# Four column tiles of 128 and one store for the output of a gated attention and feed-forward decode kernel

## The chip, the cores and the metric

The kernel runs on one core of one Trainium2 chip. The metric is the device time of one execution in microseconds (us). Most executions of one kernel agree within 0.3%, so a change of 0.2 us in 197 can be told only from several rounds in which both kernels run on the same chip, and from the durations inside a trace. "Slow state" means an execution in which the records show a lower granted TensorE clock over the whole span and a longer time; here it happened once (217.08 us at a mean clock of 0.585). The granted clock is the share of full speed at which TensorE was allowed to run.

The engines are TensorE (PE; its weight loads are listed as PEld), VectorE (DVE), ScalarE (ACT), GpSimd (POOL) and SyncE (SP). SP and ACT also issue DMAs; their sequencers are listed as SPq and ACTq. Sixteen DMA engines move the data.

## The reference, cut to what matters

Four tokens (one per batch entry) go through two paths, which are mixed by a gate.

```python
def reference(A_x, A_k_cache, A_v_cache, A_wq, A_wo, B_x, B_W_gate, B_W_up, B_W_down, gate_w):
    x = A_x                                            # [4, 1, 512] bfloat16
    g = _sigmoid((x * gate_w).sum(-1, keepdims=True))
    a = _A_ref(x, A_k_cache, A_v_cache, A_wq, A_wo)    # 32 heads of 128 over the last 4096 keys; o @ wo, wo [4096, 512]
    b = _B_ref(x, B_W_gate, B_W_up, B_W_down)          # (relu(gate) * up) @ W_down, W_down [1792, 512]
    return g * a + (1 - g) * b                         # [4, 1, 512]
```

The kernel reads 81 MB (64 MB of it keys and values) to produce 4 KB of output. The parts that matter here are the last two products, `h @ W_down` and `o @ wo`. They are summed in the same PSUM accumulator, whose 4 x 512 results are cast to bfloat16 and stored.

## The kernel before: the parts that the change touches

The loads are issued by SP in one order: query weights, keys and values of eight sets, gate and up weights, the last values, down weights, and at the end the 4 MB of `wo` in six pieces. The 512 output columns are cut in two tiles of 256. Tile j is computed in TensorE's columns 64j and lands in partitions 64j to 64j+3. Both tiles run side by side.

```python
WO_PIECES = ((0, 8), (8, 16), (16, 24), (24, 28), (28, 30), (30, 32))   # 3 x 1 MB, 512 KB, 2 x 256 KB
OUTT = 2
OW = 512 // OUTT          # 256 columns of a tile
OR = 128 // OUTT          # tile j at partition 64*j

def store(E, e, t):       # tile t: 4 neighbouring partitions, 4 rows of 512 B
    E.op(lambda: e.dma_start(out.rearrange("b o d -> (b o) d")[:, OW * t:OW * t + OW], osum[OR * t:OR * t + 4, :]),
         ev=("OUT", t), waits=[("OSUM",)], ctr=f"d_out{t}")

# ... cut ...  TensorE: FFN (down projection) and WO (output projection) into bank ACC
def WO(p):
    lo, hi = WO_PIECES[p]
    w = [("WO", p)] + [("E", "OQ", g) for g in range(2)]
    for i in range(lo, hi):
        for j in range(OUTT):
            mm(banks[ACC][OR * j:OR * j + 4, 0:OW], oq[:, i, :], Wo[:, i, OW * j:OW * j + OW], False, i == 31,
               ev=..., waits=w if (i, j) == (lo, 0) else (), pos=(0, OR * j))

# ... cut ...  VectorE, last instruction
def FIN():
    E.op(lambda: v.tensor_copy(osum[:, :], banks[ACC][:, 0:OW]), ev=("OSUM",), waits=[("WOP", len(WO_PIECES) - 1)])

# ... cut ...  SP stores tile 0, ACT stores tile 1
```

## Time and profile before

| before | us |
|---|---|
| time, median of 3 runs | 197.54 |
| last `wo` load lands | 192.84 |
| last four matmuls | 192.89 to 193.27 |
| cast to `osum` | 193.31 to 193.74 |
| stores land (trace's increments): SP's, ACT's | 194.95, 195.13 |
| span ends | 195.59 |

The page of the kernel before shows what bounds it. Its third part lists the DMA queues with packets, MB and their share of the time of sixteen engines; its fourth part is the chain of work that ended last.

```profile
## 3 DMA queue, kind: packets, MB, share of 16 engines
q1 hardware_dynamic: 3904, 81.01, 97.1%
...
DMA 54%; DVE 30%; PE 9%; issue 5%; SPq 1%; ACT 0%
```

The load queue fills 97.1% of sixteen DMA engines' span. There is hardly any room in front of the last load, so what a change of the output path can win lies behind it. The end of the chain of waits in the same run, in order of time (start, duration, what), shows that part:

```profile
173.35 19.49 DMA slots<-in_A_wo_dram
192.84 0.04 issue
192.89 0.40 PE bank L320 x4
193.29 0.02 issue
193.31 0.42 DVE osum L576
```

The chain stops at the cast. The stores follow in the timeline of the same run (start, duration, engine, line, instruction). For a DMA the duration is the time the sequencer needs to issue it:

```profile
193.77 0.29 SPq L249 DMA_DIRECT2D out_dram<-osum  x1
193.77 0.62 ACTq L249 DMA_DIRECT2D out_dram<-osum  x1
```

Both stores are alike, and ACT takes twice as long to issue its one. So after the last load there are 2.75 us: 0.47 to the cast, 0.43 of cast, 1.39 to the last store's landing, 0.46 to close the program.

One more thing is read from the trace's packet records. Each DMA increments its semaphore once for each engine that takes part. For the last piece of `wo` these increments come in two groups:

```text
increments of the last piece, us after the first (190.98):
0.00 0.05 0.10 0.17 0.26 0.28 0.29 0.47 0.48 0.57 | 1.44 1.62 1.70 1.74 1.76 1.87
```

Six engines are late. Five 16 KB instruction fetches before the end (at 39, 72, 111, 146 and 183 us) each hold one engine for 0.92 to 1.06 us, and after each fetch one more engine is late in every later load. The sixth late engine appears after a single 8 KB fetch at 64 us. The loads are cut evenly, so nothing gives that time back. A load is complete when its slowest engine is.

### The profile page before, as it was taken

To read this page: it belongs to the slowest core of one execution; us is meant where nothing else is said; L and a number is where in the kernel's file an instruction comes from. 1 tells how busy PE (TensorE), PEld (TensorE's weight loads), DVE (VectorE), ACT (ScalarE), POOL (GpSimd) and SP (SyncE) were. 2 spreads that over 40 slices of the span, in tenths; PEclk is the share of its full clock that TensorE was granted. 3 is DMA by queue.
4 is the path that set the end of the run, shared out by engine and by line. 5 is a ranking of instruction groups with operands and counts; after the bars stand their busy time and mean duration, and the time that the engine had idled before them with its cause. 6 is when DMAs were issued, how large, how long until landed. Compare 5 with 4: busy or idle time off the path is not lost.

```text
span 195.6 us, 1780 instructions
## 1 busy us (share of the span) xinstructions
PE 121.2 (62%) x741; PEld 50.9 (26%) x741; DVE 124.0 (63%) x153; ACT 27.3 (14%) x33; POOL 9.5 (5%) x25
## 2 busy tenths in 40 slices
PE   0418279465933894595468953893395557734954
PEld 0213123122411331142113521241141112412631
DVE  6104769999299819971998199819972997460000
ACT  2213000040130013001300131014001400420100
POOL 7830000000000000000000000000000000000000
PEclk9999957999999697999886999699999789997999
DMA  6999999999999999999999999999999999999991
GB/s 221 442 423 436 429 442 436 419 436 429 436 456 429 437 426 436 429 429 429 436 429 436 426 429 429 429 429 429 429 426 429 429 405 434 448 429 403 417 402 53
DMA packets 3919, 81.12 MB, mean 415 GB/s; under 512 B 572, under 2 KB 584, under 8 KB 968
## 3 DMA queue, kind: packets, MB, share of 16 engines
q1 hardware_dynamic: 3904, 81.01, 97.1%
q8 instruction: 6, 0.10, 0.2%
q14 instruction: 1, 0.01, 0.0%
q10 hardware_dynamic: 8, 0.00, 0.0%
HBM read 81.01 MB, written 0.00 MB: 414 GB/s over the span
## 4 chain that ended last, share of the span: by engine, by line
DMA 54%; DVE 30%; PE 9%; issue 5%; SPq 1%; ACT 0%
DMA slots<-in_A_k_cache_dram 38%; DVE kt L492 21%; DMA slots<-in_A_wo_dram 10%; PE bank L320 7%; DMA gwT<-in_gate_w_dram 6%; DVE sc L528 5%; DVE qblk L518 1%; SPq L256 1%; DVE pT L543 1%; PE bank L324 1%; DVE rd L532 1%; ACT gwB L598 0%; DVE negmax L538 0%; DVE oq L555 0%; DVE osum L576 0%
## 5 line engine op out<-in xcount | busy, mean ns | idle before, releaser
L492 DVE STREAM_TRANSPOSE kt<-slots 128x2048 f32<-128x2048 f32 x32 | 73.7, 2304 | 27.5 <-DMA slots<-in_A_k_cache_dram 27.5
L320 PE MATMUL bank<-kt,qblk 128*128 128x512 bf16 x256 | 71.4, 430 | 29.2 <-DVE kt L492 29.1
L320 PEld LDWEIGHTS bank<-kt,qblk 128*128 128x128 bf16 x256 | 24.9, 106 | 70.7 <-DVE kt L492 37.6
L320 PE MATMUL bank<-slots,pT 128*64 128x512 bf16 x256 | 32.0, 407 | 5.7 <-DMA slots<-in_A_v_cache_dram 5.7
L617 ACT ACTIVATE pe<-sc,negmax 128x2048 bf16<-128x2048 bf16 x8 | 16.0, 2002 | 60.3 <-DVE negmax L538 60.3
L528 DVE CUSTOM_DVE_ANT_0 sc<-bank,maskf 128x512 bf16<-128x512 f32 x32 | 21.1, 658 | 4.1 <-PE bank L320 4.1
L320 PEld LDWEIGHTS bank<-slots,pT 128*64 128x64 bf16 x256 | 15.0, 117 | 23.1 <-issue 13.1
L543 DVE STREAM_TRANSPOSE pT<-pe 128x2048 bf16<-128x2048 bf16 x8 | 18.5, 2312 | 2.2 <-ACT pe L617 2.2
L602 ACT ACTIVATE osb<-bank 128x512 bf16<-128x512 f32 x8 | 4.8, 597 | 81.5 <-PE bank L320 81.5
L320 PE MATMUL bank<-rd,grpb 128*128 128x32 bf16 x8 | 1.5, 192 | 21.0 <-DVE rd L532 19.3
L555 DVE TENSOR_TENSOR oq<-bank,recip 64x128 bf16<-64x128 f32 x2 | 0.9, 442 | 11.5 <-PE bank L320 11.4
L320 PEld LDWEIGHTS bank<-rd,grpb 128*128 128x128 bf16 x8 | 0.8, 97 | 24.7 <-DVE rd L532 22.7
L320 PE MATMUL bank<-slots,oq 128*4 128x256 bf16 x64 | 4.3, 272 | 2.6 <-DMA slots<-in_A_wo_dram 1.9
L496 DVE COPY xT<-bank 128x16 bf16<-128x16 bf16 x1 | 0.2, 167 | 8.2 <-PE bank L324 8.2
L320 PE MATMUL bank<-slots,xT 128*4 128x512 bf16 (+1 forms) x64 | 5.2, 483 | 0.0
L576 DVE CAST osum<-bank 128x256 bf16<-128x256 f32 x1 | 0.4, 425 | 6.5 <-PE bank L320 6.5
L518 DVE TENSOR_SCALAR qblk<-bank 32x64 uint32<-32x64 uint32 x16 | 2.9, 215 | 2.3 <-PE bank L324 2.2
L320 PE MATMUL bank<-maskr,maskl 128*128 128x512 bf16 x1 | 0.6, 609 | 5.9 <-POOL maskr L296 5.9
L324 PE MATMUL bank<-identb,xsb 4*128 4x4 bf16 x4 | 0.3, 166 | 5.4 <-DMA xsb<-in_A_x_dram 5.4
L320 PEld LDWEIGHTS bank<-slots,oq 128*4 128x4 bf16 x64 | 2.3, 83 | 4.4 <-DMA slots<-in_A_wo_dram 3.1
L296 POOL TENSOR_SCALAR_AFFINE_SELECT fold<-fold 128x256 bf16<-128x256 bf16 x8 | 3.3, 417 | 1.1
L487 DVE MEMSET qblk<- 128x2304 uint32 x1 | 2.0, 1978 | 1.4 <-PEq L640 1.4
(58 smaller groups left out, 42.2 us busy)
## 6 DMA issues: line engine op xcount, KB each, us to landing
slots<-in_A_k_cache_dram SPq DMA_DIRECT2D x8, 4096.0 KB, 25.2
slots<-in_A_v_cache_dram SPq DMA_DIRECT2D x8, 4096.0 KB, 30.6
slots<-in_A_wq_dram SPq DMA_DIRECT2D x1, 4096.0 KB, 12.4
slots<-in_A_wo_dram SPq DMA_DIRECT2D x3, 1024.0 KB, 16.4
slots<-in_B_W_gate_dram SPq DMA_DIRECT2D x1, 1792.0 KB, 19.7
slots<-in_B_W_up_dram SPq DMA_DIRECT2D x1, 1792.0 KB, 23.6
slots<-in_B_W_down_dram SPq DMA_DIRECT2D x1, 1792.0 KB, 18.6
slots<-in_A_wo_dram SPq DMA_DIRECT2D x1, 512.0 KB, 19.2
```

The costliest lines, as they stand in the source:

```text
L256: E.op(lambda: e.dma_start(dst, src), ev=ev, waits=waits, ctr=ctr)
L296: op(lambda: e.affine_select(dst, src, pattern, cmp, fill, base=base, channel_multiplier=mult), ev)
L320: E.op(lambda: t.matmul(out_, lhsT, rhs, start=start, stop=stop, tile_position=pos, skip_group_check=True), ev=ev, waits=waits)
L324: E.op(lambda: t.transpose(out_, in_, idn), ev=ev, waits=waits)
L487: E.op(lambda: v.memset(qblk[:, :, :, :, :].rearrange("p s h c e -> p (s h c e)"), 0.0), ev=("QZ",))
L492: E.op(lambda: v.transpose(kt[:, f, :].bitcast(FP32), slot("k", s)[:, 4096 * f:4096 * f + 4096].bitcast(FP32)), ev=("E", "KT", s, f), waits=w)
L518: E.op(lambda dst=dst, r=r, g=g: v.tensor_scalar(dst, src[r, g, 0:B, :, :], 0, None, op0=ALU.bitwise_or), ev=("E",) + keys[1] if (q, g) == ...
L528: E.op(lambda: v.tensor_tensor_reduce(sc[:, 512 * f:512 * f + 512], banks[scb(key)], R["maskf"][:, :], 1.0, -3.0e38, ALU.add, ALU.max, mx4 ...
L532: E.op(lambda: v.tensor_tensor(rd32[:, :, :], bc(R["own8"][:, :].unsqueeze(2), 2, 4), bc(mx4[:, :].unsqueeze(1), 1, 8), ALU.mult), ev=("MA ...
L543: E.op(lambda: v.transpose(pT[:, s % 2, :], pe[:, :]), ev=("E", "PT", s), waits=[("EXP", s)] + ([("PV", s - 2)] if s >= 2 else []))
L602: E.op(lambda: a.activation(osb[:, s % 4, :], ob(s), ACTF.Copy), ev=("NORM", s), waits=[("PV", s)] + ([("OQ", 0)] if s >= 4 else []))
L617: E.op(lambda: a.activation(pe[:, :], sc[:, :], ACTF.Exp, bias=negmax[:, s % 2:s % 2 + 1], scale=SCALE, accum_out=rowsum[:, s:s + 1]), ev= ...
```

## The change

The intent: shorten everything behind the last load. Four column tiles of 128 columns make the last matmuls and the cast half as wide. The rows of a tile lie 8 partitions apart, so that all 16 rows have one step (`osum[0:128:8]`) and a single store takes them. The last 64 KB of `wo` are loaded in rows of 123, 3 and 2, numbers that three, three and two DMA engines can share, so that the late engines have nothing to do with them. The rest follows from it: one second-level head sum instead of two, memsets for the unused columns, bfloat16 constants.

```diff
-WO_PIECES = ((0, 8), (8, 16), (16, 24), (24, 28), (28, 30), (30, 32))
-OUTT = 2
+OUTT = 4
 OW = 512 // OUTT
 OR = 128 // OUTT
+ST = OR // B
+LW = 3 * ST + 2
+WO_PIECES = ((0, 32), (32, 64), (64, 96), (96, 112), (112, 120), (120, 126), (126, 128))
+LOW3 = (0, 123, 126, 128)
@@ loads
-                load(("WO", it[1]), f"d_wo{it[1]}", Wo[:, lo:hi, :], A_wo.rearrange("(p i) c -> p i c", i=32)[:, lo:hi, :],
-                     waits=w)
+                wo = A_wo.rearrange("(p i) c -> p (i c)", i=32)
+                for n, r in enumerate(wo_rows(it[1])):      # last piece: rows 0:123, 123:126, 126:128
+                    load(("WO", it[1], n), f"d_wo{it[1]}", Wo[r, OW * lo:OW * hi], wo[r, OW * lo:OW * hi], waits=w)
@@ stores
-        for t in range(0, OUTT, 2):
-            store(E, e, t)
-        E.wait([("OUT", t) for t in range(OUTT)])
+        load(("OUT",), "d_out", out.rearrange("b o (t c) -> t (b o) c", t=OUTT),
+             osum[0:128:ST, :], waits=[("OSUM",)])
+        E.wait([("OUT",)])
@@ TensorE
-                    mm(banks[ACC][OR * j:OR * j + 4, 0:OW], R["hg"][:, i, :], Wd[:, x:x + OW], i == 0, False,
+                    mm(banks[ACC][OR * j:OR * j + LW, 0:OW], R["hg"][:, i, :], Wd[:, x:x + OW], i == 0, False,
-            for i in range(lo, hi):
-                for j in range(OUTT):
-                    mm(banks[ACC][OR * j:OR * j + 4, 0:OW], oq[:, i, :], Wo[:, i, OW * j:OW * j + OW], False, i == 31,
+            for x in range(lo, hi):
+                i, j = x // OUTT, x % OUTT
+                mm(banks[ACC][OR * j:OR * j + LW, 0:OW], oq[:, i, :], Wo[:, OW * x:OW * x + OW], False, i == 31,
@@ cut: one OQ and EOQ pair instead of two, memsets of hg and oq, ee and e4 in BF16, ACT's store removed
```

More of the change, by code (lines that the diff above doesn't have):

```diff
@@ L116, in _alloc @@
     sb("gwT", [128, 4], BF16)
-    sb("osb", [128, 4, 512], BF16)
-    sb("oq", [128, 32, 4], BF16)
+    sb("osb", [128, NSET, 512], BF16)
+    sb("oq", [128, 32, LW], BF16)
     sb("identb", [128, 128], BF16)
@@ L121, in _alloc @@
     sb("ones", [128, 128], FP32)
-    sb("ee", [16, 128], FP32)
-    sb("e4", [16, 128], FP32)
+    sb("ee", [16, 128], BF16)
+    sb("e4", [16, 128], BF16)
     sb("rfold", [128, 128], FP32)
@@ L136, in _alloc @@
     sb("rowsum", [128, NSET], FP32)
-    sb("recip", [128, 2, 4], FP32)
+    sb("recip", [128, 4, 4], FP32)
     sb("ge", [128, 2, 4], FP32)
@@ L140, in _alloc @@
     sb("gg", [128, 2, 4], FP32)
-    sb("hg", [128, 14, 4], BF16)
+    sb("hg", [128, 14, LW], BF16)
     sb("osum", [128, OW], BF16)
@@ L150, in _order @@
     for s in range(1, NSET):
-        o += [("KT", s, 0), ("SC", s - 1, 3)] + [("RS", 0), ("OQ", 0)] * (s == 5) + [("SW", s - 1)]
+        o += [("KT", s, 0), ("SC", s - 1, 3)] + [("RS", 0)] * (s == 5) + [("SW", s - 1)]
         o += [("KT", s, 1), ("PT", s - 1), ("SC", s, 0), ("KT", s, 2), ("SC", s, 1), ("KT", s, 3)]
@@ L154, in _order @@
     s = NSET - 1
-    o += [("SC", s, 3), ("SW", s), ("PV", s - 1), ("PT", s), ("RS", 1), ("GU",), ("PV", s), ("FFN",), ("OQ", 1)]
+    o += [("SC", s, 3), ("SW", s), ("PV", s - 1), ("PT", s), ("RS", 1), ("GU",), ("PV", s), ("FFN",), ("OQ",)]
     return o + [("WO", p) for p in range(len(WO_PIECES))]
@@ L207, in _program @@
     Wd = slot("wd")[:, 0:14 * 512]
-    Wo = slot("wo", 0).rearrange("p (i c) -> p i c", i=32)
+    Wo = slot("wo", 0)
     grelu, hrow, hT = sc[:, 0:448], sc[:, 512:960], sc[:, 1024:1472]
@@ L240, in sc_free, with wo_rows @@
         return [("E",) + sck[n]] if n >= 0 else [("INIT",)]
+    def wo_rows(p):
+        return [slice(a, b) for a, b in zip(LOW3, LOW3[1:])] if p == len(WO_PIECES) - 1 else [slice(0, 128)]
     def set_of(s):
@@ L246, in ob @@
         return banks[OB[s % 2]]
-    def store(E, e, t):
-        E.op(lambda: e.dma_start(out.rearrange("b o d -> (b o) d")[:, OW * t:OW * t + OW], osum[OR * t:OR * t + 4, :]),
-             ev=("OUT", t), waits=[("OSUM",)], ctr=f"d_out{t}")
     def sync(e):
@@ L310, in gpsimd @@
         aff(R["own8"][:, :], R["own8"][:, :], [[16, 8]], 15, ge_, 0.0, ("OWN", 1), mult=-1)
+        op(lambda: e.memset(R["hg"][:, :, :], 0.0), ("HG0",))
+        op(lambda: e.memset(oq[:, :, :], 0.0), ("OQ0",))
         op(lambda: e.memset(R["fold"][:, :, :, :], 0.0), ("FOLD0",))
@@ L393, in PV, with OQ @@
                        (f, c) in ((3, 12), (3, 14)), ev=("PV", s) if (f, c) == (3, 14) else None, waits=w, pos=(0, r))
-        def OQ(g):
-            key = ("OQ", g)
-            r = 64 * g
+        def OQ():
+            key = ("OQ",)
             for t in range(2):
@@ L402, in OQ @@
                         first, lastmm = (t, cc, c) == (0, 0, 0), (t, cc, c) == (1, 1, 3)
-                        mm(banks[tr(key)][r:r + 64, 0:128], R["fold"][:, 2 * cc + t, c, :], osb[:, :, x:x + 32], first,
-                           lastmm, ev=key if lastmm else None, pos=(0, r),
-                           waits=tr_free(key) + [("NORM", 4 * g + 3), ("FOLD", 7)] if first else ())
+                        mm(banks[tr(key)][0:64, 0:256], R["fold"][:, 2 * cc + t, c, :], osb[:, :, x:x + 32], first, lastmm,
+                           ev=key if lastmm else None, pos=(0, 0),
+                           waits=tr_free(key) + [("NORM", NSET - 1), ("FOLD", 7)] if first else ())
         def GU():
@@ L426, in WO @@
             lo, hi = WO_PIECES[p]
-            w = [("WO", p)] + [("E", "OQ", g) for g in range(2)]
-            for i in range(lo, hi):
-                for j in range(OUTT):
-                    mm(banks[ACC][OR * j:OR * j + 4, 0:OW], oq[:, i, :], Wo[:, i, OW * j:OW * j + OW], False, i == 31,
-                       ev=("WOP", p) if (i, j) == (hi - 1, OUTT - 1) else None, waits=w if (i, j) == (lo, 0) else (),
-                       pos=(0, OR * j))
+            w = [("WO", p, n) for n in range(len(wo_rows(p)))] + [("E", "OQ")]
+            for x in range(lo, hi):
+                i, j = x // OUTT, x % OUTT
+                mm(banks[ACC][OR * j:OR * j + LW, 0:OW], oq[:, i, :], Wo[:, OW * x:OW * x + OW], False, i == 31,
+                   ev=("WOP", p) if x == hi - 1 else None, waits=w if x == lo else (), pos=(0, OR * j))
         fns = dict(CONST=CONST, XT=XT, Z=Z, Q=Q, QT=QT, SC=SC, PV=PV, SW=SW, RS=RS, OQ=OQ, WO=WO, GU=GU, FFN=FFN)
@@ L470, in _program @@
         elif k == "OQ":
-            dve.append(("EOQ", it[1]))
+            dve.append(("EOQ",))
     dve.append(("FIN",))
@@ L547, in ERS, with EOQ @@
             key = ("RS", g)
-            E.op(lambda: v.reciprocal(recip[:, 0, :], banks[tr(key)][:, 0:4]), ev=("E",) + key, waits=[key])
-            E.op(lambda: v.tensor_tensor(recip[:, 1, :], recip[:, 0, :], gg[:, 0, :], ALU.mult), ev=("RG", g),
+            E.op(lambda: v.reciprocal(recip[:, 2 * g, :], banks[tr(key)][:, 0:4]), ev=("E",) + key, waits=[key])
+            E.op(lambda: v.tensor_tensor(recip[:, 2 * g + 1, :], recip[:, 2 * g, :], gg[:, 0, :], ALU.mult), ev=("RG", g),
                  waits=[("E",) + key, ("G",)])
-        def EOQ(g):
-            key = ("OQ", g)
-            r = slice(64 * g, 64 * g + 64)
-            E.op(lambda: v.tensor_tensor(oq[r, :, :].rearrange("p i b -> p b i"),
-                                         banks[tr(key)][r, 0:128].rearrange("p (b i) -> p b i", b=4),
-                                         bc(recip[r, 1, :].unsqueeze(2), 2, 32), ALU.mult), ev=("E",) + key,
-                 waits=[key, ("RG", g)])
+        def EOQ():
+            key = ("OQ",)
+            for g in range(2):
+                r = slice(64 * g, 64 * g + 64)
+                E.op(lambda g=g, r=r: v.tensor_tensor(
+                    oq[r, :, 0:LW:ST].rearrange("p i b -> p b i"),
+                    banks[tr(key)][0:64, 128 * g:128 * g + 128].rearrange("p (b i) -> p b i", b=4),
+                    bc(recip[0:64, 2 * g + 1, :].unsqueeze(2), 2, 32), ALU.mult), ev=("E",) + key if g else None,
+                    waits=[key, ("RG", 1), ("OQ0",)])
         def H():
@@ L570, in EHT @@
             E.op(lambda: v.transpose(hT, hrow), ev=("HT",), waits=[("H",)])
-            E.op(lambda: v.tensor_tensor(R["hg"][:, :, :], hT.rearrange("p (i b) -> p i b", b=32)[:, :, 0:4],
+            E.op(lambda: v.tensor_tensor(R["hg"][:, :, 0:LW:ST], hT.rearrange("p (i b) -> p i b", b=32)[:, :, 0:4],
                                          bc(gg[:, 1, :].unsqueeze(1), 1, 14), ALU.mult), ev=("E", "HT"),
-                 waits=[("HT",), ("G",)])
+                 waits=[("HT",), ("G",), ("HG0",)])
         def FIN():
@@ L601, in NORM @@
         def NORM(s):
-            E.op(lambda: a.activation(osb[:, s % 4, :], ob(s), ACTF.Copy), ev=("NORM", s),
-                 waits=[("PV", s)] + ([("OQ", 0)] if s >= 4 else []))
+            E.op(lambda: a.activation(osb[:, s, :], ob(s), ACTF.Copy), ev=("NORM", s),
+                 waits=[("PV", s)])
         def GE():
@@ L622, in scalar @@
             fns[it[0]](*it[1:])
-        for t in range(1, OUTT, 2):
-            store(E, a, t)
     return [("tensor", tensor), ("vector", vector), ("scalar", scalar), ("gpsimd", gpsimd), ("sync", sync)]
```

## The prediction

> **What bounds the kernel.** The DMA stream: the page's queue section gives the load queue 97.1% of sixteen engines' span. The chain that ended last, from 165 us on, is 62.9% output-weight loads. Compute hides behind the loads, so only the tail can change:
> - The last output-weight piece lands at 192.84 (chain of waits).
> - Four matmuls of 256 columns: 192.89 to 193.27, 0.40 in the chain.
> - The output cast, 128x256: 193.31, 0.42.
> - Two stores from 193.77: issue 0.29 on SP, 0.62 on ACT. In the trace's DMA increments SP's lands at 194.95, ACT's at 195.13. The span ends at 195.59.
>
> **How the stream ends.** The last piece's increments come in two groups: ten engines at 190.98 to 191.55, six at 192.42 to 192.85. In the packet records each 16 KB instruction fetch (39, 72, 111, 146, 183 us) holds one engine 0.9 to 1.05 us; after it one more engine is late in every later load. So ten engines idle about 1.3 us at the end.
>
> **What the change does there.**
> 1. Rows of 123, 3, 2. The Trainium skill ("DMA: Bandwidth & Descriptors", why a DMA increments its semaphore by 16) says the engine count is the largest number up to 16 that divides the slowest dimension, lowest-numbered engines first. So 123 rows go to three engines, 41 rows of 512 B each, then three, then two. No run shows this yet. The other thirteen lose 4 KB each: eight packets shrink from 2048 B (80 ns apart) to 1536 B (about 61 ns), 0.15 us. The three get about 43 packets at an estimated 22 to 28 ns, about 1 us, into 1.3 us of slack, if they are early engines. My packet matching suggests so, not surely.
> 2. Last piece: two matmuls of 128 columns side by side instead of two pairs of 256. The second pair starts 105 ns after the first; a 128-column one lasts 219 ns in the trace: 0.16 less.
> 3. Cast of 128 columns instead of 256, at about 1 ns each: 0.13 less.
> 4. One store, not two: ACT's landed 0.19 after SP's. Against it: 16 rows of 256 B, and the skill's page (Specifications) warns of read-modify-write below 512 B. Net 0.07 less.
>
> **What is added off the critical path.** FFN and output matmuls double (28 to 56, 64 to 128). Gate and up projections ran four column tiles with starts 3 ns apart, 189 ns per group of 448 columns, so four at 128 columns should cost 56 to 90 ns against 108 for today's pair. The merged head fold costs 0.8 more, its second scaling 0.44; output matmuls still start near 188 and catch up before the third piece lands at 190.34. Three more load issues (0.43 each) hide behind 19 us of queueing; constants and memsets come early.
>
> **Sum.** 0.15 + 0.16 + 0.13 + 0.07 = 0.5 us less: 197.05 us (196.6 to 197.65). Faster over 2%: 1%; within 2%: 97%; slower: 2%.
>
> **What would show it.** Last landing near 192.7; last matmuls about 0.23; cast about 0.29; one store; increments of the last piece from three engines only, none later than the six late ones.
>
> **What would make it wrong.** The three being late ones, or 512-byte packets slower than 28 ns: the last landing moves up to 1 us. More TensorE instructions bring the next fetch forward (191.5 to about 189); on one of the three or on a late engine it costs up to 1 us. Slow 256-byte writes eat the store's gain.

## The result, and the profile after

The changed kernel took 197.64 us (median of 6 runs, 197.58 to 197.86), the kernel before 197.47 us in the same rounds (197.31 to 197.91). The ratio is 1.0006 with a 95% interval of 0.9993 to 1.0019. Ratios in this document are made from the fast runs of both kernels in the same rounds. They are not quite the ratio of the medians quoted; the plain means of the listed times give the same within 0.0005. In a second series of 5 rounds the ratio was 1.0015 (1.0002 to 1.0027). So there is no gain. If anything the change costs 0.1 to 0.3 us, and the time lies at the very upper end of the predicted range (197.64 of 197.65).

The page after shows the stream as it was:

```profile
## 3 DMA queue, kind: packets, MB, share of 16 engines
q1 hardware_dynamic: 4052, 81.01, 96.8%
```

The end of the chain of waits of the changed kernel:

```profile
172.57 19.33 DMA slots<-in_A_wo_dram
191.90 0.04 issue
191.95 0.61 PE bank L326 x16
192.56 0.01 issue
192.57 0.40 PE bank L326 x8
192.97 0.03 issue
193.00 0.45 PE bank L326 x8
193.45 0.02 issue
193.47 0.29 DVE osum L582
```

The cast fell from 0.42 to 0.29 as intended. But the matmuls before it take 0.45, not less than the 0.40 of before, and eight of them wait for the last landing, not two. Then the store, from the timeline:

```profile
193.79 0.67 SPq L259 DMA_DIRECT2D out_dram<-osum  x1
```

Its issue takes 0.67 where SP's plain store took 0.29. Laid out from the landing of the last down weights, which both kernels load alike, the tails are as follows (from the traces' increments and instruction times; the second run of the changed kernel is the control of the first experiment):

| us | before | after | after, again | predicted change |
|---|---|---|---|---|
| down weights landed to last `wo` landing | 9.97 | 9.93 | 10.02 | -0.15 |
| last landing to start of cast | 0.47 | 0.52 | 0.42 | -0.16 |
| cast | 0.43 | 0.29 | 0.29 | -0.13 |
| cast to last store's landing | 1.39 | 1.78 | 1.77 | -0.07 with the next row |
| landing to end of span | 0.46 | 0.40 | 0.40 | |
| sum | 12.72 | 12.93 | 12.91 | -0.5 |

Only the cast is as predicted. The first two rows together, from the down weights to the start of the cast, are 10.44 before and 10.45 and 10.44 after: nothing of the 0.31 us forecast for them came. The store is the largest difference: 0.39 worse where a little gain was forecast.

### The profile page after: what moved, and what is told of

Read it like the earlier page. It is cut to its first block, busy times and chain, and to the rows that moved or that the text cites. A ratio compares the mean times of both kernels' runs of the same rounds, so it can differ in the third digit from the quotient of the medians.

```text
span 195.9 us, 1933 instructions
## 1 busy us (share of the span) xinstructions
PE 119.7 (61%) x815; PEld 50.1 (26%) x815; DVE 124.5 (64%) x153; ACT 27.1 (14%) x33; POOL 10.7 (5%) x27
## 3 DMA queue, kind: packets, MB, share of 16 engines
q1 hardware_dynamic: 4052, 81.01, 96.8%
## 4 chain that ended last, share of the span: by engine, by line
DMA 58%; DVE 29%; PE 6%; issue 4%; SPq 1%
DMA slots<-in_A_k_cache_dram 49%; DVE kt L496 21%; DMA slots<-in_A_wo_dram 10%; PE bank L326 6%; DVE sc L532 5%; DVE pT L547 1%; SPq L259 1%; DVE rd L536 1%; DVE negmax L542 0%; DVE osum L582 0%; DVE mx L532 0%; DVE recip L553 0%; DVE recip L552 0%
## 5 line engine op out<-in xcount | busy, mean ns | idle before, releaser
L326 PE MATMUL bank<-kt,qblk 128*128 128x512 bf16 x256 | 73.5, 441 | 24.2 <-DVE kt L496 24.2
L326 PEld LDWEIGHTS bank<-kt,qblk 128*128 128x128 bf16 x256 | 25.8, 109 | 67.5 <-DVE kt L496 31.8
L326 PE MATMUL bank<-slots,pT 128*64 128x512 bf16 x256 | 31.5, 403 | 5.7 <-DMA slots<-in_A_v_cache_dram 5.7
L326 PE MATMUL bank<-slots,oq 128*26 128x128 bf16 x128 | 3.1, 240 | 3.7 <-DMA slots<-in_A_wo_dram 2.1
L326 PEld LDWEIGHTS bank<-slots,oq 128*26 128x26 bf16 x128 | 2.0, 98 | 4.9 <-DMA slots<-in_A_wo_dram 3.0
L542 DVE TENSOR_REDUCE negmax<-bank 128x1 f32<-128x32 f32 x8 | 1.5, 192 | 2.0 <-PE bank L326 2.0
```

The costliest lines, as they stand in the source:

```text
L326: E.op(lambda: t.matmul(out_, lhsT, rhs, start=start, stop=stop, tile_position=pos, skip_group_check=True), ev=ev, waits=waits)
L542: E.op(lambda: v.tensor_reduce(negmax[:, s % 2:s % 2 + 1], banks[tr(key)][:, 0:32], AXIS.X, ALU.min), ev=("E",) + key, waits=[key])
```

## The experiments

Theory A: the one store gives back what the rest gains. Theory B, the rival: the split of the last load slows the stream. Both were put to the chip, and then their parts.

### The changed kernel again, as control

> The changed kernel once more, as the control of this call. Theory A (the one store gives back what the tail gains): 197.5 to 197.8 us, 0.0 to 0.3 slower than before; SP issue of the store 0.67 us, last store landing 1.75 us after the cast ends, against 0.29 and 1.36 before. Theory B (the split load lets the stream end later): last output-weight landing at least 0.1 us later than before, counted from the end of the same stream.

No edit. It took 197.67 us against 197.32 for before, ratio 1.0015 (1.0002 to 1.0027). The store's issue was 0.66 us, and it landed 1.77 us after the cast. The last landing, counted from the down weights, was 0.05 us later than before in this run and 0.04 earlier in the first. Theory A's numbers hold; theory B's 0.1 does not show. One thing differs between the two runs. In the first the rows on three engines were done 0.47 us before the piece of 192 KB on sixteen; in this one they landed 0.10 us after it, and were the last landing. In both the cast began 0.52 us after the piece of 192 KB.

### The last 64 KB in one load

> The changed kernel with its last 64 KB of output weights in one load of 128 rows. Theory A: about the same as the changed kernel (within 0.15 us): the last landing comes up to 0.2 later, but then only the last two matmuls wait for it instead of eight. Theory B: 0.15 us or more faster than the changed kernel. If the split worked as intended: 0.15 us slower.

```diff
-LOW3 = (0, 123, 126, 128)
+LOW3 = (0, 128)
```

197.38 us, ratio to before 1.0008 (0.9994 to 1.0022), against 1.0015 for the control of the same rounds. The median is 0.29 us under the control's. Five runs each, which spread over 0.60 and 0.45 us, can't tell this from none, so the times alone don't decide between A and B. In the trace the last landing was 10.02 us after the down weights. Only two matmuls waited for it, and the cast began 0.37 us after it instead of 0.42 to 0.52. From the down weights to the start of the cast it is 10.40 us, against 10.45 and 10.44 with the split. So what the split gains in landing, the matmuls behind it lose again, as theory A had it; for theory B 0.05 us are left.

### The store cut in two, SP and ACT

> The changed kernel with the one store cut in two, column tiles 0 and 1 from SP, 2 and 3 from ACT. Theory A with a cost by number of rows: SP issue near 0.45 us, landing 0.2 earlier than the one store, but ACT's 0.7 to 0.8 lands last, so the time stays within 0.1 of the changed kernel. If the cost is of the three-dimensional pattern and not of its rows: SP issue stays 0.6 to 0.67. Theory B: no effect on anything before the stores, time within 0.1.

```diff
-        load(("OUT",), "d_out", out.rearrange("b o (t c) -> t (b o) c", t=OUTT), osum[0:128:ST, :], ...)
+        half(E, e, 0)            # SP: tiles 0 and 1, osum[0:64:ST]
+    # end of ACT's program
+        half(E, a, 1)            # ACT: tiles 2 and 3, osum[64:128:ST]
```

197.76 us, ratio 1.0018 (1.0006 to 1.0031). From its timeline:

```profile
192.96 0.29 PE L329 MATMUL bank<-slots,oq 128*26 128x128 bf16 x8
193.33 0.29 DVE L585 CAST osum<-bank 128x128 bf16<-128x128 f32 x1 [3.68 <-PE bank L329]
193.65 0.64 SPq L256 DMA_DIRECT2D out_dram<-osum  x1
193.65 1.37 ACTq L256 DMA_DIRECT2D out_dram<-osum  x1
```

Half the rows take SP 0.64 us, nearly as long as all of them (0.67). So the issue time does not go with the number of rows. ACT needs 1.37 for its half, more than the 0.7 to 0.8 I had expected.

The first line is a find by chance. Here eight matmuls took 0.29 us. The same eight of the changed kernel took 0.40; from the start of the first to the cast it is 0.37 against 0.48. The view by windows (busy time with instruction counts per engine, then the granted clock) shows why. First the changed kernel, then this one:

```profile
188.30:191.70 3.40, 1.59 (x96) 1.23 (x88) 0.00 (x0) 0.00 (x0) 0.00 (x0) 1.00 0.88 332
191.70:193.60 1.90, 1.41 (x32) 0.61 (x32) 0.13 (x1) 0.00 (x0) 0.00 (x0) 0.51 0.09 32
```

```profile
188.30:191.70 3.40, 1.52 (x96) 1.37 (x96) 1.33 (x2) 0.00 (x0) 0.00 (x0) 1.00 0.89 336
191.70:193.60 1.90, 0.99 (x32) 0.46 (x32) 0.27 (x1) 0.00 (x0) 0.00 (x0) 1.00 0.09 31
```

And the kernel before, in the same two stretches:

```profile
188.30:191.70 3.40, 1.72 (x30) 0.96 (x26) 0.00 (x0) 0.00 (x0) 0.00 (x0) 1.00 0.84 327
191.70:193.60 1.90, 1.29 (x16) 0.37 (x16) 0.28 (x1) 0.00 (x0) 0.00 (x0) 1.00 0.10 39
```

In the changed kernel TensorE's clock was at half in the tail (0.51 in the last column but two). The Trainium skill, "TensorE: Matmul & The Clock Gate", Part 1, says that the clock falls back to half after an idle window of about 3.4 us, and that these windows run freely. The length fits the clock records of this trace: the last stretch at full clock runs from 181.50 to 191.74, three times 3.41 us. But the last of these three windows was not idle: in the stretch shown, nearly the same, TensorE was busy 1.59 us. Nor does the busy time of one window decide it. The kernel before kept its clock after 1.72 us in that stretch, and the kernel with two stores, busy only 1.52 us in nearly the same window (188.19 to 191.61), kept it too, while the one with one load of 64 KB lost it after 1.62. With two stores the window before had been busy 3.38 us, in the changed kernel 1.78, and the full clock had begun one window later than there; whether that is the reason was not tested. The clock fell before the last matmuls in the profiles of five kernels with four column tiles (the changed kernel twice). It held in the one above and in one whose waits are filled with matmuls, below. What sets it stays open.

### The kernel before with one store

> The kernel before, with its two column tiles written 16 partitions apart and stored at once by SP (8 rows of 512 B, three-dimensional on the HBM side), nothing else changed. Theory A: SP issue 0.45 to 0.67 us, store lands 0.1 to 0.3 later than before's ACT store, time 0.0 to 0.3 us slower than before. If only the 256-byte rows made the store slow: issue 0.3, landing 0.19 earlier than before's later store, 0.2 us faster than before. Theory B says nothing of it: same as before.

```diff
+ST = OR // B              # 16
+LW = 3 * ST + 2
-                    mm(banks[ACC][OR * j:OR * j + 4, 0:OW], oq[:, i, :], ...
+                    mm(banks[ACC][OR * j:OR * j + LW, 0:OW], oq[:, i, :], ...      # rows 16 partitions apart
-        for t in range(0, OUTT, 2): store(E, e, t)        # and ACT's for t = 1
+        load(("OUT",), "d_out", out.rearrange("b o (t c) -> t (b o) c", t=OUTT), osum[0:128:ST, :], waits=[("OSUM",)])
```

197.78 us, ratio to before 1.0023 (1.0011 to 1.0036), about 0.45 us slower. From the timeline:

```profile
194.42 0.64 SPq L258 DMA_DIRECT2D out_dram<-osum  x1
```

This is the store of the change put alone into the kernel before, with the wider spacing of rows that it needs, and it costs. The issue is 0.64 us though the rows are 512 B long, and the store lands 1.75 us after the cast instead of 1.39. That is 0.36 of the 0.45 us. The cast began 0.03 us later, counted from the down weights. So short rows are not what makes the store slow, and half as many rows do not make it fast.

### The stores by themselves

Two kernels run further stores at the end of the changed kernel, each waiting for the one before, and leave the right result last.

> The changed kernel followed by eight more stores, each waiting for the one before (SP: the store of the change; 16 rows of 256 B one after the other in HBM; 4 rows of 256 B; the change's pattern from 16 neighbouring partitions; two tiles of the change's pattern; 4 rows of 512 B; ACT: the change's store; 4 rows of 512 B; SP: the change's store again; the last one leaves the right result). If the three-dimensional HBM side costs the issue time (theory A1): 0.64 to 0.67 us on SP for every such pattern whatever its rows and partitions, 0.29 to 0.33 for both two-dimensional ones, also with 16 rows; on ACT 1.3 to 1.4 against 0.62. If the number of rows does (A2): 16 rows in two dimensions also take 0.6 or more, and two tiles less than four. If the partition step of 8 does (A3): neighbouring partitions bring 0.3.

> The changed kernel with other stores around its own, each waiting for the one before, after the stores of the first such run fell together at 0.56 to 0.67 us on SP whatever their dimensions, but 0.28 for 4 neighbouring rows of 512 B. In order on SP: 4 neighbouring rows of 512 B; the same of 256 B; 4 rows of 512 B from partitions 8 apart; 8 neighbouring rows of 512 B in the three-dimensional order; 8 in two dimensions; 4 rows of 1 KB; 4 of 512 B again; then ACT twice 4 neighbouring rows of 512 B; SP the change's store. If a partition step above 1 is the slow thing: 0.6 for the third and the last, 0.3 for the others. If short rows are: 0.6 for the second and the last. If the three-dimensional side is: 0.6 for the fourth. If more than four rows are: 0.6 for fourth and fifth. ACT: 0.62 the first time, 0.31 the second, if its first store is slow for being the first.

```diff
+        for n in range(10):
+            if n not in (7, 8):          # 7 and 8 are issued by ACT
+                probe(E, e, n)           # waits for ("OUT", n - 1)
```

In the first of them everything with rows 8 partitions apart took 0.56 to 0.67 us on SP, also 4 rows and also a two-dimensional store (0.64 and 0.58); neighbouring partitions with the three-dimensional order took 0.66. So none of its three theories was right alone. The second one parts them. From its timeline, one line for each store, in the order of the expectation:

```profile
193.53 0.27 SPq L270 DMA_DIRECT2D out_dram<-slots  x1
194.71 0.26 SPq L270 DMA_DIRECT2D out_dram<-slots  x1
195.88 0.73 SPq L270 DMA_DIRECT2D out_dram<-slots  x1
197.68 0.68 SPq L270 DMA_DIRECT2D out_dram<-slots  x1
199.46 0.29 SPq L270 DMA_DIRECT2D out_dram<-slots  x1
200.69 0.25 SPq L270 DMA_DIRECT2D out_dram<-slots  x1
201.93 0.25 SPq L270 DMA_DIRECT2D out_dram<-slots  x1
203.11 0.55 ACTq L270 DMA_DIRECT2D out_dram<-slots  x1
204.34 0.26 ACTq L270 DMA_DIRECT2D out_dram<-slots  x1
205.52 0.58 SPq L270 DMA_DIRECT2D out_dram<-osum  x1
```

Read it line by line. Four neighbouring rows take 0.25 to 0.27 us to issue, whether of 256 B, 512 B or 1 KB, and eight take 0.29. The same four rows from partitions 8 apart take 0.73. Neighbouring rows with a three-dimensional side in HBM take 0.68. Each of the two conditions is enough by itself, and having both, as the change does, is no worse than one (0.58 to 0.67). The landing follows 0.88 to 0.97 us after the issue of SP's plain stores and 1.04 to 1.18 after that of the slow ones. That is the 0.39 us of the table: 0.38 more of issue than SP's plain store (0.67 against 0.29) and 0.20 more behind it, less the 0.18 us by which before waits for ACT's later store.

The Trainium skill, "DMA: Bandwidth & Descriptors", Specifications, names 512 B as the smallest transfer at full rate and a read-modify-write below it. No penalty shows here: 4 rows of 256 B landed 0.89 us after their issue, 4 of 512 B 0.90 us. My prediction had named that warning as the risk, and it was not what made the store slow.

The ACT lines show why ACT's store of before took 0.62. The first one is slow (0.55), the second, equal one takes 0.26, as SP's do.

### TensorE kept busy in its waits

> The changed kernel with 14 idle-time matmuls (128x512 into a bank that is free) put into the waits of TensorE between the second-level sum and the fourth output-weight piece. If the halved clock in the tail costs the matmul gain: the clock stays at 1.0 to the end, the last group of matmuls takes 0.22 to 0.30 us from first start to end instead of 0.32 to 0.40, time 0.1 us less than the changed kernel, still not faster than before by more than 0.1. If the clock is not it: no change.

```diff
+            FILL({("OQ",): 5, ("WO", 1): 5, ("WO", 2): 3, ("WO", 3): 1}.get(it, 0))    # n matmuls 128x512 into bank 2
```

197.64 us, ratio 1.0009 (0.9995 to 1.0022). The clock stayed at 1.0 until past the end, but the filling was too much:

```profile
192.48 0.41 PE L326 MATMUL bank<-slots,oq 128*26 128x128 bf16 x16
193.14 0.41 PE L326 MATMUL bank<-slots,oq 128*26 128x128 bf16 x16 [0.25 <-issue]
```

The last landing was at 192.78, and the last sixteen matmuls began only at 193.14. What the clock gained was lost to that.

> The first such run kept the clock but its filling matmuls ran into the fourth piece and held TensorE 0.36 us past the last landing. Here fewer, in the same four column tiles as the output matmuls: four groups of 512 columns after the second-level sum, four after the second piece, two after the third. If the halved clock costs: clock 1.0 to the end, last matmuls done 0.30 us after the last landing instead of 0.40 (as in the run with two stores, whose clock happened to hold), TensorE not late, time 0.1 us under the changed kernel's 197.64. If not: 197.6 to 197.7.

```diff
+            FILL({("OQ",): 4, ("WO", 1): 4, ("WO", 2): 2}.get(it, 0))    # groups of four column tiles of 512
```

197.82 us, ratio of the fast runs 1.0012 (0.9998 to 1.0026). The profiled execution fell into the slow state (217.08 us, mean clock 0.585), so its trace says nothing here, and the fast runs scatter from 197.35 to 197.99. This one failed to measure what it was for. That the halved clock costs 0.1 us of matmul time therefore rests on the two traces above (0.40 against 0.29 for the same eight matmuls). That holding the clock shortens the kernel is not shown.

### Only the split, in the kernel before

> The kernel before with only the last 64 KB of output weights split into rows of 123, 3 and 2 (one piece of 192 KB before it). As intended: last 16-engine landing 0.15 us earlier, counted from the landing of the FFN down weights (9.83 instead of 9.98), time 0.1 to 0.15 us less. Theory B (the 512-byte packets slow the other engines): less than 0.08 of it left. The prediction's error would then be in that term too.

```diff
-WO_PIECES = ((0, 8), (8, 16), (16, 24), (24, 28), (28, 30), (30, 32))
+WO_PIECES = ((0, 16), (16, 32), (32, 48), (48, 56), (56, 60), (60, 63), (63, 64))    # in half rows of 256 columns
+LOW3 = (0, 123, 126, 128)
```

197.28 us, ratio 0.9997 (0.9984 to 1.0009). The last landing was 9.93 us after the down weights, 0.04 less than before. The split does what it should, and does not harm, but the gain is a third of the 0.15 predicted. The increments show where the rest goes. The fourth piece (512 KB, cut alike in all these kernels) landed 1.25 to 1.28 us after the third in the five kernels without the split, and 1.33 to 1.42 us after it in the eight profiles with it (the slow one left out). Seven of these thirteen:

| us, last landing after the third piece's | before | one store | short tail | one load | only the split | after | after, again |
|---|---|---|---|---|---|---|---|
| split | no | no | no | no | yes | yes | yes |
| fourth piece | 1.25 | 1.26 | 1.27 | 1.28 | 1.37 | 1.39 | 1.35 |
| last load on 16 engines | 2.51 | 2.54 | 2.58 | 2.57 | 2.48 | 2.44 | 2.47 |

The packets of 512 B of the three engines run in just that stretch: in the changed kernel they start at 190.35 to 191.50, and the fourth piece lands at 191.90. They take 27 ns each in the median. So theory B has a small truth: about 0.1 us of what the split gains is lost in the piece before. By what means the late engines are slowed was not tested and stays open.

### A shorter tail with plain stores

> The kernel before with its stores kept two-dimensional, the output halves in two PSUM banks so that DVE and ACT cast 128 columns each at the same time, and the last output-weight piece halved (128 KB). If the tail of compute is what can be gained and the stores must stay as they were: cast 0.43 to 0.30, last matmuls 0.38 to 0.29, in all 0.15 to 0.2 us less than before; stores as before (SP issue 0.29, ACT 0.62). If it isn't: no change.

```diff
-WO_PIECES = (..., (28, 30), (30, 32))
+WO_PIECES = (..., (28, 30), (30, 31), (31, 32))
+HW = OW // 2
+OUTB = (5, 2)                            # columns 0:128 of each tile in bank 5, 128:256 in bank 2
-    v.tensor_copy(osum[:, :], banks[ACC][:, 0:OW])
+    v.tensor_copy(osum[:, 0:HW], banks[OUTB[0]][:, 0:HW])                  # DVE
+    a.activation(osum[:, HW:OW], banks[OUTB[1]][:, 0:HW], ACTF.Copy)       # ACT, at the same time
```

197.27 us, ratio 0.9994 (0.9981 to 1.0006). The cast took 0.29 instead of 0.43 and began 0.36 us after the last landing instead of 0.47, so 0.24 us of the tail went. The stores stayed as they were, but both wait for two casts now, and one more piece makes the stream end 0.07 us later. From the down weights to the end of the span it is 12.59 us against 12.72. That is too small to be told from the noise of the times.

> The kernel before with the short tail (two banks, two casts, smaller last piece) and one early ACT store of 4 rows to the output's second half, done near 186 us and written over by the real one. If ACT's store takes 0.62 us to issue only for being ACT's first: 0.31 now, its landing 0.18 earlier and even with SP's, time 0.25 to 0.35 us less than before and 0.15 less than the short tail alone. If ACT is slower in general: issue 0.62, time as the short tail alone (0.05 to 0.1 less than before).

```diff
+        # ACT, after its last copy at 184.9 us
+        a.dma_start(out.rearrange("b o d -> (b o) d")[:, OW:2 * OW], xsb[0:4, 0:OW])    # written over by the real store
+        E.wait([("EARLY",)])
```

```profile
184.86 0.55 ACTq L629 DMA_DIRECT2D out_dram<-xsb  x1
...
193.34 0.29 DVE L581 CAST osum<-bank 128x128 bf16<-128x128 f32 x1 [5.37 <-PE bank L322]
193.40 0.28 ACT L632 ACTIVATE osum<-bank 128x128 bf16<-128x128 f32 x1 [7.95 <-PE bank L322]
193.76 0.26 ACTq L251 DMA_DIRECT2D out_dram<-osum  x1
193.76 0.29 SPq L251 DMA_DIRECT2D out_dram<-osum  x1
```

197.09 us (197.06 to 197.22) against 197.45, ratio 0.9983 (0.9968 to 0.9997). ACT's store is issued in 0.26 us nine microseconds after the early one took 0.55. So its first DMA is slow for being the first. But only the issue is shown to be shorter. This is the one kernel whose interval lies below 1 against before, and its median is 0.5 us under the changed kernel's, though of other rounds. I would not lean on its last tenth: of its forecast, the store's landing did not hold. The two stores now start together on the same engines, SP's lands at 195.10, and the step from cast to landing is 1.42 us where it was 1.44 in the short tail alone. And in its trace the time from the down weights to the end of the span is 12.74 us, not less than the 12.72 of before, because the last landing came 0.25 us later (10.22 instead of 9.97). So where its 0.3 us come from is not shown.

### The change with plain stores

> The changed kernel with the rows of its four column tiles next to each other again (partitions 32t to 32t+3) and four plain stores of 4 rows, two from SP and two from ACT, ACT having made an early store near 185 us; everything else of the change kept. If the strided, three-dimensional store is what gave the change's gain back: each issue 0.26 to 0.30 us, the last landing 1.40 to 1.50 us after the cast ends instead of 1.77, time 0.25 to 0.35 us under the changed kernel (197.3 to 197.4 where it had 197.65) and even with before or up to 0.15 under it. If the gain was lost elsewhere: 197.6 or more.

```diff
-ST = OR // B
-LW = 3 * ST + 2
+ST = 1
+LW = 4
-        load(("OUT",), "d_out", out.rearrange("b o (t c) -> t (b o) c", t=OUTT), osum[0:128:ST, :], ...)
+        for t in range(0, OUTT, 2): store(E, e, t)        # SP: tiles 0 and 2; ACT, after an early store: 1 and 3
```

```profile
194.03 0.61 SPq L256 DMA_DIRECT2D out_dram<-osum  x2
194.09 0.66 ACTq L256 DMA_DIRECT2D out_dram<-osum  x2
```

197.64 us, ratio 1.0011 (0.9998 to 1.0025). This expectation failed: the time is in the range that was given for a gain lost elsewhere. But the run does not part the two, for it has a cost of its own. Each issue is short (0.26 to 0.36 us), but each engine has two of them, one after the other. The last landing is 1.72 us after the cast, hardly under the 1.77 of the strided store. So in the two arrangements tried, one slow store or two plain ones in a row on each engine cost four column tiles the same. That the slow store costs rests on the kernel before with one store, not on this run. Plain stores from a third engine were not tried.

## Why the prediction was right or wrong, point by point

- **What bounds the kernel** held: the stream is at 96.8% after, and the time moved by less than 0.2%.
- **"Cast of 128 columns instead of 256 ... 0.13 less"** held exactly: 425 to 292 ns.
- **"FFN and output matmuls double"** off the critical path held: 56 matmuls of the down projection took 0.96 us, 69 ns for a group of four, and the output matmuls began at 188.18. The Trainium skill, "TensorE: Matmul & The Clock Gate", Part 3, says that column tiles run at the same time, and the trace agrees: the four tiles of a group start 3 ns apart.
- **The instruction fetch** came at 191.0 instead of 191.5, not at 189, and cost nothing that the increments of the changed kernel show.
- **Step 4, "One store, not two ... Net 0.07 less"**, is the step that failed most. Cast to landing took 1.78 us instead of 1.39, with 0.06 won back at the end: 0.33 worse instead of 0.07 better. I had asked whether short rows would be slow to write. The cost was in the issue, 0.67 instead of 0.29, and in 0.20 more from there to the landing, because the rows are 8 partitions apart and because the HBM side has three dimensions. The store put into the kernel before (ratio 1.0023) and the ten lines of stores show it.
- **Step 2, "Last piece: two matmuls ... 0.16 less"**, failed. The prediction had two matmuls waiting for the last landing, at full clock. It took the last landing for the one awaited and did not follow the piece of 192 KB before it. That piece, on sixteen engines, lands at the end too, so eight matmuls stand behind it, and TensorE's clock had fallen to half by then. The cast began 0.52 us after this piece in both runs, where 0.31 (0.47 less 0.16) had been forecast. The runs part the two causes: eight matmuls at full clock (two stores) made it 0.41, and two at half clock (one load of 64 KB) 0.37.
- **Step 1, "Rows of 123, 3, 2 ... 0.15"** was right in mechanism, but little of it remained. The increments come from three, three and two engines, as the skill's rule ("DMA: Bandwidth & Descriptors", why a DMA increments its semaphore by 16) says. Which engines these are the records don't tell. The last landing on sixteen engines followed the one before after 0.42 us instead of 0.62. But the fourth piece took 0.1 us longer, and 0.04 to 0.05 remained. The 1.3 us of slack for the three engines was no safe margin: they were done 0.47 us before the others in one run and 0.10 us after them in the next.
- The sum missed for these three terms: steps 1 and 2 together gave 0.00 instead of 0.31, and step 4 0.33 more instead of 0.07 less. The range held only because it reached up to no gain at all, and by 0.01 us: that was luck, and not the argument.

## What to carry to other kernels

At the end of this kernel a store's issue counted in full: keep its rows in neighbouring partitions and its HBM side two-dimensional, for here either a partition step or a third dimension took 0.3 to 0.5 us more, which is more than the shorter cast won (0.13). An engine whose last store is its first DMA can issue some DMA earlier: here that made the issue 0.3 us shorter, though the landing hardly moved. And ask of a tail which piece lands last and how many instructions wait for it; a clever last piece did nothing here while the one before it was the one awaited.

## What the Trainium skill lacked or had wrong

- "DMA: Bandwidth & Descriptors" has no figure for what the shape of a DMA costs the issuing sequencer on this chip: 0.25 to 0.30 us on SP for 4 or 8 neighbouring rows, 0.56 to 0.73 us on SP with a partition step of 8 or 16, or with a three-dimensional HBM side.
- The same page has nothing on the first DMA of an engine: ACT took 0.55 to 0.62 us for its first plain store and 0.26 to 0.36 us for later ones; 1.10 and 1.37 us where the first one was a strided store.
- The same page warns of a read-modify-write below 512 B; 4 rows of 256 B landed 0.89 us after their issue, 4 rows of 512 B 0.90 us, so nothing of it shows at this size.
- Neither that page nor "Runtime: NRT & Kernel Launch" has what an instruction fetch costs a stream of loads: each 16 KB fetch held one engine 0.9 to 1.1 us, and in the kernel before six of sixteen engines ended 1.4 to 1.9 us behind the first.
- "TensorE: Matmul & The Clock Gate", Part 1, ties the fall to half clock to an idle window; here it fell after 3.4 us in which TensorE was busy 1.59 us, and stayed up after 1.72 us and, in another kernel, after 1.52 us.
- "SBUF — State Buffer" has no figure for what a strided write costs VectorE: the scaling of `oq` took 442 ns with its elements written 8 B apart and 718 ns with 52 B (4 and 26 bfloat16 elements), and again 434 ns with 8 B in the change with plain stores.
